# Sliding-window attention with a leaky-ReLU feed-forward: the probability adds go to the front of each step, the key placements behind

## The chip, the core and the metric

The kernel runs on one core of one Trainium2 chip. The core has five engines with a queue each: TensorE (PE, whose weight loads have a row of their own, PEld), VectorE (DVE), ScalarE (ACT), GpSimd (POOL) and SyncE (SP), which here only issues loads. An engine works through its queue in the order in which the program was written, and waits on semaphores for the others. The metric is the device time of one execution in microseconds (us). A profiled execution gives a span, from its first to its last instruction, and a device time that is a little longer.

## What is computed

Eight batches of eight heads attend over 576 tokens, each token to those at most 32 positions away. The heads are laid side by side into 4608 rows of 512, and these go through two matrix products with a leaky ReLU between.

```python
def _attn_ref(q, k, v):                       # 8, 8, 576, 64
    scores = np.matmul(q, k.transpose(0, 1, 3, 2)) / np.sqrt(D)
    mask = np.abs(pos[:, None] - pos[None, :]) <= 32
    scores = np.where(mask, scores, -1000000000.0)
    attn = np.exp(scores - np.max(scores, axis=-1, keepdims=True))
    attn = attn / (np.sum(attn, axis=-1, keepdims=True) + 1e-09)
    return np.matmul(attn, v)

def _moe_ref(x, w_in, w_out):                 # 4608x512, 512x2048, 2048x512
    h = x @ w_in
    return np.maximum(0.01 * h, h) @ w_out
```

## The kernel before, in words

Two heads make a pair, so a batch has four pairs (p = 0 to 3). The work on attention is cut into 64 units, numbered i: batch b = i // 8, half of the tokens hf = (i // 4) % 2, pair p = i % 4. For every unit there are three stages.

- `score(i)`: five matmuls of PE into the one PSUM tile `ps`, with the pair's keys as weights (`kbd`) and its queries `qT` streaming; then ACT takes the exponential into `e`, and POOL multiplies by the band mask into `pr`.
- `join(i)`: two instructions of DVE that add the two parts of `pr` into `both` (L239 and L241). Units below 12 have no join; their sums take two matmuls instead of one.
- `weighted(i)`: PE sums the probabilities into `s` (from `both`, L250) and forms the weighted values `x` (from `pr` and the block-diagonal values `vbd`, L262). Then DVE takes the reciprocal of `s` (L268, `r`) and multiplies it into `x` (L270), which gives a piece of `xT`. `s` and `x` have one PSUM buffer each.

A batch reaches that form in steps that belong to the batch before it. q and k are loaded by SP, cast to bf16 (`cast_qk`, into `qb` and `kb`), transposed by six small matmuls of PE into `tp` (L185), and copied out by ACT to `qT` (L193) and `kT` (L199). Two copies of DVE, one for each head of the pair, then place `kT` into the block-diagonal `kbd` (L202). `kbd` and `vbd` have two buffers, for even and odd batches; `kT` has two. `transposes(b)` is a generator of eight pieces (q0, k0, q1, k1, ...), and a piece of k ends with its placement.

The feed-forward is two kinds of tile: `h_tile(g, f)`, four matmuls (L281) and a leaky ReLU by ACT, over 288 tokens; and `o_tile(j)`, sixteen matmuls of 512 columns (L298) for 128 tokens, copied out by ACT and stored. Both take their PSUM tiles from a ring of four, which `tp` shares.

Nothing but the written order sets what stands behind what. `step()` writes one unit: a piece of the next batch's transposes, `score(i + 2)`, `weighted(i)`, `join(i + 1)`, another piece of the transposes, and then casts and loads for later batches. Which pieces, casts and loads belong to which unit of a batch is in the table `PLAN`. For batches from 2 on the last piece, k3, is transposed in the first unit of the batch itself, ahead of `score` and `weighted`; in batch 1 most of the pieces fall into its last units. A plan of due times puts the steps between the h and o tiles. Two stretches are written out by hand: the first batch, and the second one's preparation, which runs beside `h_tile(0, f)` and `h_tile(1, f)`. There the four query casts of batch 1 stand on DVE one after another, the key casts on POOL, and after every fourth `h_tile(1, f)` a pair's two pieces are transposed; `score(8)` and `score(9)` follow when all is done, and then the first o tile.

Of the kernel before, what the change touches and what calls it, by code (L numbers as in the profile page):

```python
# [10 lines left out]
BF16 = mybir.dt.bfloat16  # L11
# [5 lines left out]
def kernel(  # L17
# [12 lines left out]
    nc = tc.nc  # L30

    B, H, S, D = q.shape
# [5 lines left out]
    NPAIR = H // 2  # L38
# [9 lines left out]
    fload = ctx.enter_context(tc.tile_pool(name="fload", bufs=1))  # L48
    cast = ctx.enter_context(tc.tile_pool(name="cast", bufs=1))
    attn = ctx.enter_context(tc.tile_pool(name="attn", bufs=2))  # L50
    prob = ctx.enter_context(tc.tile_pool(name="prob", bufs=4))
    outp = ctx.enter_context(tc.tile_pool(name="outp", bufs=4))
    PS = bass.MemoryType.PSUM
# [8 lines left out]
    def load_qk(b, p, behind=None):  # L62


        for into, src, name in ((qf, q, "qf"), (kf, k, "kf")):
            t = fload.tile([96, 2, RUN * D], FP32, name=f"{name}{p}")
            if behind is not None:
                nc.sync.dma_start(out=t[0:1, 0, 0:1], in_=behind.bitcast(FP32))
                behind = None
            nc.sync.dma_start(  # L70
                out=t, in_=src[b, p:H:NPAIR].rearrange("a (p c) d -> p a (c d)", c=RUN),
            )
            into[b, p] = t
# [37 lines left out]
    kbd = [const.tile([128, NPAIR, NB, 128], BF16, name=f"kbd{i}") for i in range(2)]  # L111
    vbd = [const.tile([128, NPAIR, NB, 128], BF16, name=f"vbd{i}") for i in range(2)]
# [23 lines left out]
    for lo in (0, 64):  # L136
        w = win[lo:lo + 64]
        nc.gpsimd.affine_select(
            out=w, in_=w, compare_op=ALU.is_ge, fill=0.0,
# [3 lines left out]
            out=w, in_=w, compare_op=ALU.is_ge, fill=0.0,  # L143
# [20 lines left out]
    def cast_qk(b, p, q_eng=None):  # L164
        for eng, src, dst in ((q_eng or nc.gpsimd, qf, qb), (nc.gpsimd, kf, kb)):
            eng.tensor_copy(  # L166
                out=dst[:, p], in_=src[b, p].rearrange("p a (c d) -> p c a d", d=D),
            )

    def cast_v(b, p, on_act=False):  # L170
        for a in range(2):
            r = slice(64 * a, 64 * a + 64)
            if on_act:
                nc.scalar.activation(out=vbd[b % 2][r, p, :, r], in_=vf[b, p][r], func=AF.Copy)
            else:
                nc.gpsimd.tensor_copy(out=vbd[b % 2][r, p, :, r], in_=vf[b, p][r])  # L176

    def transposes(b):

        qT[b] = attn.tile([128, NPAIR, S], BF16, name="qT")  # L180
        for p in range(NPAIR):
            for which, src in (("q", qb), ("k", kb)):
                tp = mmps.tile([128, RUN, 96], BF16, name="tp", tag="mm")
                for c in range(RUN):
                    nc.tensor.transpose(  # L185
                        tp[:, c],
                        src[:, p, c].rearrange("p a d -> p (a d)"),
                        ident[0:96, 0:96],
                    )

                tok = tp.rearrange("p c i -> p i c")
                if which == "q":
                    nc.scalar.activation(  # L193
                        out=qT[b][:, p].rearrange("p (i c) -> p i c", c=RUN), in_=tok, func=AF.Copy,
                    )
                else:
                    kT = attn.tile([128, S], BF16, name="kT")
                    kT_v = kT.rearrange("p (i c) -> p i c", c=RUN)
                    nc.scalar.activation(out=kT_v, in_=tok, func=AF.Copy)  # L199
                    for a in range(2):  # L200
                        r = slice(64 * a, 64 * a + 64)
                        nc.vector.tensor_copy(  # L202
                            out=kbd[b % 2][r, p, :, r],
                            in_=kT[r].rearrange("p (n j) -> p n j", j=64),
                        )
                yield

    probs = {}

    def where(i):  # L210
        return i // 8, (i // 4) % 2, i % 4

    def score(i):
        b, hf, p = where(i)
        ps = scps.tile([128, 1024], FP32, name="ps")
        c0 = 512 - HALF
        for blk, q0, n in WIN[hf]:
            nc.tensor.matmul(  # L218
                ps[:, c0:c0 + n], kbd[b % 2][:, p, blk],
                qT[b][:, p, q0:q0 + n], start=True, stop=True,  # L220
            )
            c0 += n
        e = attn.tile([128, NCOL], BF16, name="e")
        nc.scalar.activation(  # L224
            out=e, in_=ps[:, 512 - HALF:512 - HALF + NCOL], func=AF.Exp, scale=scale,
        )
        pr = prob.tile([128, NCOL], BF16, name="pr")
        nc.gpsimd.tensor_mul(pr, e, mask[hf])  # L228
        probs[i] = pr, None

    def join(i):


        hf = where(i)[1]
        pr = probs[i][0]
        both = prob.tile([128, HALF], BF16, name="both")
        o0 = ODD[hf]
        o1 = o0 + NCOL - HALF
        nc.vector.tensor_add(both[:, o0:o1], pr[:, o0:o1], pr[:, HALF:NCOL])  # L239
        rest = slice(0, o0) if o0 else slice(o1, HALF)  # L240
        nc.vector.tensor_copy(out=both[:, rest], in_=pr[:, rest])  # L241
        probs[i] = pr, both

    def weighted(i):
        b, hf, p = where(i)
        pr, both = probs.pop(i)
        x = xps.tile([128, HALF], FP32, name="x")
        s = xps.tile([128, HALF], FP32, name="s")
        if both is not None:
            nc.tensor.matmul(s, ones_bd, both, start=True, stop=True)  # L250
        else:
            nc.tensor.matmul(
                s, ones_bd, pr[:, 0:HALF], start=True, stop=False, skip_group_check=True,
            )
            nc.tensor.matmul(
                s[:, ODD[hf]:ODD[hf] + NCOL - HALF], ones_bd, pr[:, HALF:NCOL],
                start=False, stop=True, skip_group_check=True,
            )
        c0 = 0
        for n_, (blk, q0, n) in enumerate(WIN[hf]):  # L260
            a = q0 - HALF * hf
            nc.tensor.matmul(  # L262
                x[:, a:a + n], vbd[b % 2][:, p, blk, :], pr[:, c0:c0 + n],
                start=(n_ == 0), stop=(n_ == len(WIN[hf]) - 1), skip_group_check=True,
            )
            c0 += n
        r = attn.tile([128, HALF], FP32, name="r")
        nc.vector.reciprocal(r, s)  # L268
        t0 = (b * S + hf * HALF) % RING
        nc.vector.tensor_mul(xT[:, p, t0:t0 + HALF], x, r)  # L270
# [43 lines left out]
    NC = 2 * NPAIR * B  # L314
    JOINED = 12
# [13 lines left out]
    def step_transposes(upto):  # L329
        while state["tp"] < min(upto, 8 * B):  # L330
            b = state["tp"] // 8
            if b not in t_parts:
                t_parts[b] = transposes(b)
            next(t_parts[b])
            state["tp"] += 1

    def step():


        i = state["done"]  # L340
        b, r = i // 8, i % 8
        if b > 0:
            upto = 8 * (b + 1) + PLAN[b > 1][0][r]
            step_transposes(max(upto - 1, 8 * (b + 1)))
        if i < 7:
            score(i + 1)
        elif 8 <= i < NC - 2:
            score(i + 2)
        weighted(i)
        if JOINED - 1 <= i < NC - 1:  # L350
            join(i + 1)
        if b > 0:
            step_transposes(upto)
        if 0 < b < B - 1:
            for p in PLAN[b > 1][1][r]:
                cast_qk(b + 1, p)
                if b + 2 < B:
                    load_qk(b + 2, p)
            for p in PLAN[b > 1][2][r]:
                cast_v(b + 1, p)  # L360
                if b + 2 < B:
                    load_v(b + 2, p)
        state["done"] += 1
# [11 lines left out]
    def load_w_out(i):  # L375
        c = slice(4 * i, 4 * i + 4)
        nc.gpsimd.dma_start(out=w_out_bf[:, c, :], in_=w_out_r[:, c, :])

    first = transposes(0)

    def first_pair():
        next(first)
        next(first)

    cast_qk(0, 0, nc.vector)
    make_masks()
# [35 lines left out]
    for f in range(FFC):  # L422
# [2 lines left out]
            step()  # L425
        if f % 4 == 3:
            nc.gpsimd.memset(kbd[1][:, f // 4], 0.0)
    for p in range(NPAIR):
        cast_qk(1, p, nc.vector)
    for p in range(NPAIR):  # L430
        load_v(1, p, w_out_bf[0:1, 4, 0:2] if p == 0 else None)
    second = transposes(1)
    for f in range(FFC):
        h_tile(1, f)
        if f % 4 == 3:
            next(second)
            next(second)
            nc.gpsimd.memset(vbd[1][:, f // 4], 0.0)
    state["tp"] = 16
    score(8)  # L440
    score(9)
    for p in range(NPAIR):
        load_qk(2, p)
# [71 lines left out]
```

## Time and profile before

| | |
|---|---|
| device time, three runs | 346.3, 348.11, 348.61 us; median 348.11 |
| the profiled execution | 348.38 us, its span 346.7 us |
| busy in that span | PE 319.2, DVE 228.2, ACT 200.2, POOL 180.5 us |
| costliest groups | `h_tile` matmuls 135.7 us, `o_tile` matmuls 130.3 us, reciprocals on DVE 125.3 us |

Times in rows of a trace are counted from the span's start. A row of the timeline has the start, the time from there to the end of the last of its instructions, the engine, line, operation and names, the count, and in brackets how long the engine had stood idle before it and what released it. A row of waits has who waited for whom, the total in us, how often, and the longest.

### The profile page before, as it was taken

The numbers are of one execution on the slowest core, as the hardware profiler recorded it, in microseconds if no ns is written. First come the engines' busy times: TensorE is split into PE (matmuls) and PEld (weight loads), VectorE is DVE, ScalarE is ACT, GpSimd is POOL, SyncE is SP. The second block draws the span as 40 slices with busy tenths as digits, with TensorE's granted clock in tenths as the row PEclk, the third lists the DMA queues.
The fourth block names the chain that finished last, engine by engine and source line by source line (L and its number), as shares of the span: only waits on it lengthen the run. The fifth ranks groups of instructions, "written<-read, shape, count | busy, mean of one in ns | idle before, by whom it ended". The sixth has DMA issues, their size and how long they took to land.

```text
span 346.7 us, 6990 instructions
## 1 busy us (share of the span) xinstructions
PE 319.2 (92%) x2703; PEld 217.0 (63%) x2725; DVE 228.2 (66%) x310; ACT 200.2 (58%) x432; POOL 180.5 (52%) x213
## 2 busy tenths in 40 slices
PE   2578969999999997999999997999999998899996
PEld 1346754576765856667675765767675765667663
DVE  5489541888767787587577877787586877766200
ACT  6765772375763936557474755658484656446441
POOL 7698557757845556355364637555463644221000
PEclk9999998999999999899999999999999999999999
DMA  8999989967774435263345433463211001010102
GB/s 184 206 199 225 268 182 232 248 164 203 175 165 135 133 96 138 69 188 74 112 126 161 134 82 106 115 183 84 80 51 61 32 2 61 2 61 3 61 2 91
DMA packets 60853, 42.40 MB, mean 122 GB/s; under 512 B 39700, under 2 KB 56340, under 8 KB 60820
## 3 DMA queue, kind: packets, MB, share of 16 engines
q1 hardware_dynamic: 51204, 28.32, 35.0%
q10 hardware_dynamic: 5328, 9.44, 7.6%
q0 software_dynamic: 4288, 4.20, 7.5%
q8 instruction: 21, 0.34, 0.4%
q14 instruction: 12, 0.10, 0.1%
HBM read 36.70 MB, written 9.44 MB: 133 GB/s over the span
## 4 chain that ended last, share of the span: by engine, by line
PE 78%; DVE 8%; DMA 7%; SPq 2%; ACT 2%; issue 1%; ACTq 0%; POOL 0%; DVEq 0%
PE mm L298 35%; PE mm L281 30%; DVE r L268 4%; DMA qf<-in_q_dram 4%; PE tp L185 4%; PE x L262 4%; PE ps L218 4%; DMA kf<-in_k_dram 2%; PE s L250 2%; SPq L70 1%; SPq L81 1%; DVE xT L270 1%; DVE kbd L202 1%; DVE both L241 1%; ACT kT L199 1%
## 5 line engine op out<-in xcount | busy, mean ns | idle before, releaser
L268 DVE RECIPROCAL r<-s 128x288 f32<-128x288 f32 x64 | 125.3, 1958 | 57.1 <-PE s L250 47.4
L228 POOL TENSOR_TENSOR pr<-e,mask 128x544 bf16<-128x544 bf16 x64 | 77.6, 1213 | 119.8 <-ACT e L224 73.4
L281 PE MATMUL mm<-xT,w_in_bf 128*128 128x288 bf16 x1024 | 135.7, 288 | 1.2 <-ACT kT L199 1.2
L298 PE MATMUL mm<-w_out_bf,gT 128*128 128x512 bf16 (+2 forms) x571 | 130.3, 376 | 1.3 <-issue 0.2
L281 PEld LDWEIGHTS <-w_in_bf 128*128 128x128 bf16 x1024 | 98.7, 99 | 27.0 <-issue 2.3
L285 ACT ACTIVATE gT<-mm 128x288 bf16<-128x288 f32 x256 | 99.6, 417 | 20.9 <-PE mm L281 9.8
L298 PEld LDWEIGHTS <-gT 128*128 128x128 bf16 x592 | 56.8, 99 | 61.0 <-issue 2.1
L303 ACT ACTIVATE o_sb<-mm 128x512 f32<-128x512 f32 (+2 forms) x37 | 21.7, 586 | 85.0 <-PE mm L298 85.0
L224 ACT ACTIVATE e<-ps 128x544 bf16<-128x544 f32 x64 | 39.9, 623 | 24.2 <-PE ps L218 12.3
L202 DVE COPY kbd<-kT 64x576 bf16<-64x576 bf16 x64 | 28.4, 444 | 22.0 <-ACT kT L199 21.5
L176 POOL CAST vbd<-vf 64x576 bf16<-64x576 f32 x58 | 39.2, 675 | 2.4 <-DMA vf<-in_v_dram 0.5
L270 DVE TENSOR_TENSOR xT<-x,r 128x288 bf16<-128x288 f32 x64 | 29.3, 458 | 6.7
L166 POOL CAST kb<-kf 96x768 bf16<-96x768 f32 x32 | 27.0, 844 | 11.4 <-DMA kf<-in_k_dram 11.4
L241 DVE COPY both<-pr 128x32 bf16<-128x32 bf16 x52 | 31.6, 608 | 0.0
L218 PE MATMUL ps<-qT,kbd 128*128 128x128 bf16 (+2 forms) x320 | 26.8, 217 | 1.4 <-ACT e L224 1.4
L262 PEld LDWEIGHTS <-vbd 128*128 128x128 bf16 x320 | 21.1, 99 | 10.7 <-issue 8.6
L262 PE MATMUL x<-pr,vbd 128*128 128x128 bf16 (+2 forms) x320 | 26.2, 214 | 0.9 <-DVE xT L270 0.8
L218 PEld LDWEIGHTS <-kbd 128*128 128x128 bf16 x320 | 20.6, 101 | 8.8 <-issue 1.5
L193 ACT ACTIVATE qT<-tp 128x576 bf16<-128x576 bf16 x32 | 20.8, 650 | 7.9 <-PE tp L185 7.4
L199 ACT ACTIVATE kT<-tp 128x576 bf16<-128x576 bf16 x32 | 20.9, 654 | 4.7 <-PE tp L185 1.7
L185 PE MATMUL tp<-ident,qb 96*128 96x96 bf16 x192 | 14.5, 215 | 8.6 <-DVE qb L166 8.6
L250 PE MATMUL s<-both,ones_bd 128*128 128x288 bf16 x52 | 14.9, 286 | 6.3 <-DVE both L241 6.3
(37 smaller groups left out, 131.5 us busy)
## 6 DMA issues: line engine op xcount, KB each, us to landing
qf<-in_q_dram SPq DMA_DIRECT2D x32, 288.0 KB, 3.4
kf<-in_k_dram SPq DMA_DIRECT2D x32, 288.0 KB, 4.2
vf<-in_v_dram SPq DMA_DIRECT2D x64, 144.0 KB, 3.6
out_dram<-o_sb ACTq DMA_DIRECT2D x35, 256.0 KB, 2.5
w_in_bf<-in_moe_w_in_dram POOLq DMA_DIRECT2D x8, 256.0 KB, 6.7
w_out_bf<-in_moe_w_out_dram POOLq DMA_DIRECT2D x4, 512.0 KB, 12.8
out_dram<-o_sb ACTq DMA_DIRECT2D x1, 192.0 KB, 1.9
out_dram<-o_sb ACTq DMA_DIRECT2D x1, 64.0 KB, 1.6
```

The lines of the kernel that those rows point to most:

```text
L176: nc.gpsimd.tensor_copy(out=vbd[b % 2][r, p, :, r], in_=vf[b, p][r])
L202: nc.vector.tensor_copy(out=kbd[b % 2][r, p, :, r], in_=kT[r].rearrange("p (n j) -> p n j", j=64),)
L218: nc.tensor.matmul(ps[:, c0:c0 + n], kbd[b % 2][:, p, blk], qT[b][:, p, q0:q0 + n], start=True, stop=True,)
L224: nc.scalar.activation(out=e, in_=ps[:, 512 - HALF:512 - HALF + NCOL], func=AF.Exp, scale=scale,)
L228: nc.gpsimd.tensor_mul(pr, e, mask[hf])
L241: nc.vector.tensor_copy(out=both[:, rest], in_=pr[:, rest])
L262: nc.tensor.matmul(x[:, a:a + n], vbd[b % 2][:, p, blk, :], pr[:, c0:c0 + n], start=(n_ == 0), stop=(n_ == len(WIN[hf]) - 1), skip_group_c ...
L268: nc.vector.reciprocal(r, s)
L270: nc.vector.tensor_mul(xT[:, p, t0:t0 + HALF], x, r)
L281: nc.tensor.matmul(h[:, 0:HALF], w_in_bf[:, c, ts(f, 128)], xT[:, c, ds(t0, HALF)], start=(c == 0), stop=(c == DMC - 1),)
L285: nc.scalar.activation(out=gT[:, f, ds(t0, HALF)], in_=h[:, 0:HALF], func=AF.Prelu, alpha=0.01,)
L298: nc.tensor.matmul(o[:, lo:hi], gT[:, f, ds(128 * j % RING, 128)], w_out_bf[:, f, lo:hi], start=(f == 0), stop=(f == FFC - 1),)
```

## The change

`place_keys()` is new: a piece of k no longer ends with the two copies into `kbd` but puts its `kT` on a list, and `place_keys` writes the copies of all that is on the list. `kT` gets four buffers. In `step()` the order becomes: `join(i + 1)`, `place_keys()`, a piece of transposes, `score(i + 2)`, `weighted(i)`, `place_keys()`, the other piece.

In the second batch's preparation the casts of pairs 0 and 1 stay ahead of `h_tile(1, 0)`; those of pairs 2 and 3 move behind the placements of pairs 0 and 1. Since `cast_qk` casts q on DVE and k on POOL, a `memset` of `vbd[1]` on POOL now stands ahead of the last key cast. `score(8)` moves from the end to behind `h_tile(1, 11)`.

```diff
+    kt = ctx.enter_context(tc.tile_pool(name="kt", bufs=4))
...
-                    kT = attn.tile([128, S], BF16, name="kT")
+                    kT = kt.tile([128, S], BF16, name="kT")
...
-                    for a in range(2):
-                        r = slice(64 * a, 64 * a + 64)
-                        nc.vector.tensor_copy(
-                            out=kbd[b % 2][r, p, :, r],
-                            in_=kT[r].rearrange("p (n j) -> p n j", j=64),
-                        )
+                    unplaced.append((b, p, kT))
                 yield
+
+    unplaced = []
+
+    def place_keys():
+
+        while unplaced:
+            b, p, kT = unplaced.pop(0)
+            for a in range(2):
+                r = slice(64 * a, 64 * a + 64)
+                nc.vector.tensor_copy(
+                    out=kbd[b % 2][r, p, :, r],
+                    in_=kT[r].rearrange("p (n j) -> p n j", j=64),
+                )
...
         b, r = i // 8, i % 8
+        if JOINED - 1 <= i < NC - 1:
+            join(i + 1)
+        place_keys()
         if b > 0:
...
         weighted(i)
-        if JOINED - 1 <= i < NC - 1:
-            join(i + 1)
+        place_keys()
         if b > 0:
             step_transposes(upto)
...
     def first_pair():
         next(first)
         next(first)
+        place_keys()
...
-    for p in range(NPAIR):
-        cast_qk(1, p, nc.vector)
+    cast_qk(1, 0, nc.vector)
+    cast_qk(1, 1, nc.vector)
...
         h_tile(1, f)
         if f % 4 == 3:
+            p = f // 4
             next(second)
             next(second)
-            nc.gpsimd.memset(vbd[1][:, f // 4], 0.0)
+            place_keys()
+            if p + 2 < NPAIR:
+                cast_qk(1, p + 2, nc.vector)
+            nc.gpsimd.memset(vbd[1][:, p], 0.0)
+        if f == 11:
+            score(8)
     state["tp"] = 16
-    score(8)
     score(9)
```

The first place is DVE's queue around unit 24, the first of batch 3. The rows below are of the kernel before: the end of `weighted(23)`, `join(24)`, the placement of k3 into `kbd1`, `weighted(24)`, `join(25)`, and the reciprocal of unit 25. The numbers behind names only tell tiles apart.

```order
L270 TENSOR_TENSOR xT_142<-x_1889,r_1897 128x288
L239 TENSOR_TENSOR both_1900<-pr_1820 128x256
L241 COPY both_1900<-pr_1820 128x32
L202 COPY kbd1_126<-kT_1942 64x9x64 x2
L268 RECIPROCAL r_1964<-s_1957 128x288
L270 TENSOR_TENSOR xT_142<-x_1956,r_1964 128x288
L239 TENSOR_TENSOR both_1967<-pr_1887 128x256
L241 COPY both_1967<-pr_1887 128x32
L268 RECIPROCAL r_2036<-s_2029 128x288
```

The same place in the changed kernel, where line numbers are 9 or 10 higher and tiles have other numbers: the end of `weighted(23)`, `join(25)`, `weighted(24)`, the placement, `join(26)`, the reciprocal of unit 25.

```order
L279 TENSOR_TENSOR xT_145<-x_1895,r_1903 128x288
L248 TENSOR_TENSOR both_1938<-pr_1893 128x256
L250 COPY both_1938<-pr_1893 128x32
L277 RECIPROCAL r_1968<-s_1961 128x288
L279 TENSOR_TENSOR xT_145<-x_1960,r_1968 128x288
L212 COPY kbd1_129<-kT_1948 64x9x64 x2
L248 TENSOR_TENSOR both_2021<-pr_1958 128x256
L250 COPY both_2021<-pr_1958 128x32
L277 RECIPROCAL r_2042<-s_2035 128x288
```

What moved: the placement went from ahead of the reciprocal of unit 24 to behind its product, and the join there is that of the unit after next.

The second place is the second batch's preparation, on DVE, before: the last product of batch 0, four query casts, and the placements of the four pairs.

```order
L270 TENSOR_TENSOR xT_142<-x_519,r_528 128x288
L166 CAST qb_123<-qf0_363 96x768
L166 CAST qb_123<-qf1_368 96x768
L166 CAST qb_123<-qf2_372 96x768
L166 CAST qb_123<-qf3_376 96x768
L202 COPY kbd1_126<-kT_624 64x9x64 x2
L202 COPY kbd1_126<-kT_668 64x9x64 x2
L202 COPY kbd1_126<-kT_712 64x9x64 x2
L202 COPY kbd1_126<-kT_756 64x9x64 x2
```

And DVE at that place now.

```order
L279 TENSOR_TENSOR xT_145<-x_522,r_531 128x288
L167 CAST qb_126<-qf0_366 96x768
L167 CAST qb_126<-qf1_371 96x768
L212 COPY kbd1_129<-kT_623 64x9x64 x2
L167 CAST qb_126<-qf2_375 96x768
L212 COPY kbd1_129<-kT_669 64x9x64 x2
L167 CAST qb_126<-qf3_379 96x768
L212 COPY kbd1_129<-kT_715 64x9x64 x2
L212 COPY kbd1_129<-kT_769 64x9x64 x2
```

The placements of pairs 0 and 1 no longer stand behind the casts of pairs 2 and 3.

At the same place on POOL, before: key casts, the clearing of `vbd1`, the masks of units 8 and 9, and the first two pairs' value casts.

```order
L166 CAST kb<-kf_374 96x768
L166 CAST kb<-kf_378 96x768
L438 MEMSET vbd_128 128x1152 x4
L228 TENSOR_TENSOR pr<-e,mask_140 128x544 x2
L176 CAST vbd_128<-vf_571 64x9x64 x2
L176 CAST vbd_128<-vf_575 64x9x64 x2
```

And POOL there now.

```order
L167 CAST kb<-kf_377 96x768
L454 MEMSET vbd_131 128x1152
L167 CAST kb<-kf_381 96x768
L454 MEMSET vbd_131 128x1152 x2
L237 TENSOR_TENSOR pr<-e,mask_143 128x544
L454 MEMSET vbd_131 128x1152
L237 TENSOR_TENSOR pr<-e,mask_143 128x544
L177 CAST vbd_131<-vf_570 64x9x64 x2
L177 CAST vbd_131<-vf_574 64x9x64 x2
```

One clearing stands between the last two key casts, and the mask of unit 8 ahead of the last clearing.

## The prediction

> **What bounds the kernel now.** I read the page first: the span, the busy times, the granted clock in 40 slices, and the chain of waits by engine.
>
> ```profile
> span 346.7 us, 6990 instructions
> PE 319.2 (92%) x2703; PEld 217.0 (63%) x2725; DVE 228.2 (66%) x310; ACT 200.2 (58%) x432; POOL 180.5 (52%) x213
> ...
> PEclk9999998999999999899999999999999999999999
> ...
> PE 78%; DVE 8%; DMA 7%; SPq 2%; ACT 2%; issue 1%; ACTq 0%; POOL 0%; DVEq 0%
> ```
>
> PE carries 78% of the chain, so time can come only from PE's idle 27.5 us (346.7 - 319.2) or from stretches where its clock is low: the two slices with an 8 (slices of 8.67 us, so from 52 and from 139 us). Next the waits between 92 and 326 us, where the kernel is in its steady run; of PE's only one is long.
>
> ```profile
> PE s L250 <- DVE both L241: 6.3, 3, 2.1
> ```
>
> Three times PE waits 2.1 us for a join. DVE is busy for only 66% of the span, so it has time enough; three times the wrong thing stands first in its queue. The other idle time that the change can touch lies around the second batch (part 3).
>
> **Part 1: the join and the placement in a step.** The timeline around the first of the three, units 24 and 25:
>
> ```profile
> 130.06 0.40 PE L218 MATMUL ps<-qT,kbd 128*128 128x96 bf16 x5
> 130.30 0.29 PE L250 MATMUL s<-both,ones_bd 128*128 128x288 bf16 x1
> 134.09 0.40 PE L218 MATMUL ps<-qT,kbd 128*128 128x96 bf16 x5
> 136.59 0.28 PE L250 MATMUL s<-both,ones_bd 128*128 128x288 bf16 x1 [2.09 <-DVE both L241]
> ...
> 131.07 0.65 ACT L199 ACTIVATE kT<-tp 128x576 bf16<-128x576 bf16 x1 [0.47 <-PE x L262]
> ...
> 127.51 1.21 POOL L228 TENSOR_TENSOR pr<-e,mask 128x544 bf16<-128x544 bf16 x1 [3.02 <-issue]
> ...
> 131.75 0.91 DVE L202 COPY kbd<-kT 64x576 bf16<-64x576 bf16 x2 [2.32 <-ACT kT L199]
> 132.69 1.96 DVE L268 RECIPROCAL r<-s 128x288 f32<-128x288 f32 x1
> ...
> 135.13 0.28 DVE L239 TENSOR_TENSOR both<-pr 128x256 bf16<-128x256 bf16 x1
> 135.33 1.21 DVE L241 COPY both<-pr 128x32 bf16<-128x32 bf16 x1
> 136.91 1.96 DVE L268 RECIPROCAL r<-s 128x288 f32<-128x288 f32 x1 [0.37 <-PE s L250]
> ```
>
> The sum of unit 24 was there from 130.30, but DVE's queue held the placement, which waited for ACT's `kT` until 131.72. So the reciprocal began at 132.69, the join of unit 25 ended at 136.54, and PE stood.
>
> Now with the new order. The mask product for unit 25 ends at 127.51 + 1.21 = 128.72. Its join, which now stands in front, takes 0.20 to the start of its second instruction and 1.21 for that, at the longest seen here, so it is done by 130.2. The reciprocal follows the sum by 0.32 (136.59 to 136.91): 130.62. From a reciprocal's start to the next thing after the product are 2.44 (132.69 to 135.13): the two placements run from 133.06 to 133.97. `score(27)`, which needs them, came at 134.09, 0.12 later. So the cover of the late placement is thin, and I cost it at nothing with a bound of 0.5 us each (an instruction of DVE more ahead of it). The join of unit 25 is then long done, and PE's wait is gone. `join(26)` ends by 135.4 (133.97 + 0.20 + 1.21), up to 0.7 after the reciprocal of unit 25 could begin; PE next asks for that product in unit 26, a step later, so this lies beside PE's tiles. Gain: 3 x 2.09 = **6.3 us**.
>
> Does the join in front cost anything elsewhere? Only where a mask product comes later than the sum of the unit before. The tightest of units 12 to 62, by going through them all, is at the end:
>
> ```profile
> 310.61 1.21 POOL L228 TENSOR_TENSOR pr<-e,mask 128x544 bf16<-128x544 bf16 x1 [2.84 <-ACT e L224]
> ...
> 312.91 0.29 PE L250 MATMUL s<-both,ones_bd 128*128 128x288 bf16 x1
> ```
>
> It ends at 311.82, 1.09 ahead of the sum. So the joins stay hidden by PE's own work. DVE's order is otherwise as it was: reciprocal, product, join.
>
> **Part 2: the clock after a stall.** The table by stretches, 2 us each, in the two low slices of the clock. Its columns are the length, the busy time and count of PE, PEld, DVE, ACT and POOL, then the granted clock, the DMA share and GB/s:
>
> ```profile
> 52.00:54.00 2.00, 1.78 (x6) 0.71 (x5) 0.08 (x1) 0.62 (x1) 2.00 (x3) 0.50 1.36 193
> 54.00:56.00 2.00, 2.00 (x8) 0.81 (x7) 0.00 (x0) 0.00 (x0) 1.94 (x4) 0.70 1.06 239
> 136.00:138.00 2.00, 1.41 (x16) 1.12 (x16) 1.63 (x2) 0.49 (x1) 2.00 (x3) 0.78 0.77 243
> 138.00:140.00 2.00, 2.00 (x10) 1.30 (x9) 1.61 (x4) 0.98 (x3) 0.04 (x1) 0.50 0.83 216
> 140.00:142.00 2.00, 2.00 (x16) 1.50 (x15) 0.00 (x0) 1.23 (x3) 0.00 (x0) 0.87 0.31 79
> ```
>
> The lost clock is 1.41 x 0.22 + 2 x 0.50 + 2 x 0.13 = **1.6 us** here and 1.78 x 0.50 + 2 x 0.30 = **1.5 us** at 52 to 56, which part 3 includes. Both follow an idle PE, and there is no third after 22 us, though the other two stalls of 2.1 us drew none. Without the idle time I take both back; the other end is nothing.
>
> The Trainium skill ("TensorE: Matmul & The Clock Gate", Part 1) says that the clock halves after an idle window of some 3.4 us and that the window runs freely. The 0.50 agrees; the stall of 2.09 us is shorter than that window, and the trace lowers the clock all the same, once in three.
>
> **Part 3: the second batch.** The timeline from 45.98 to 59.21, engine by engine, and at the end four rows of the chain of waits in order of time (start, time, what):
>
> ```profile
> 45.98 1.64 PE L281 MATMUL mm<-xT,w_in_bf 128*128 128x288 bf16 x12
> 48.83 0.65 PE L281 MATMUL mm<-xT,w_in_bf 128*128 128x288 bf16 x4 [1.22 <-ACT kT L199]
> 51.64 0.51 PE L218 MATMUL ps<-qT,kbd 128*128 128x96 bf16 x5 [1.41 <-ACT e L224]
> 51.95 0.63 PE L298 MATMUL mm<-w_out_bf,gT 128*128 128x512 bf16 x1
> ...
> 59.21 0.40 PE L262 MATMUL x<-pr,vbd 128*128 128x96 bf16 x5
> ...
> 48.12 0.65 ACT L199 ACTIVATE kT<-tp 128x576 bf16<-128x576 bf16 x1 [1.54 <-DVE kbd L202]
> ...
> 46.63 0.56 DVE L166 CAST qb<-qf 96x768 bf16<-96x768 f32 x1 [2.95 <-DMA qf<-in_q_dram]
> 47.11 2.78 DVE L202 COPY kbd<-kT 64x576 bf16<-64x576 bf16 x6
> ...
> 48.02 0.82 POOL L166 CAST kb<-kf 96x768 bf16<-96x768 f32 x1 [2.37 <-DMA kf<-in_k_dram]
> 48.79 4.05 POOL L438 MEMSET vbd<- 128x1152 bf16 x4
> 52.81 2.38 POOL L228 TENSOR_TENSOR pr<-e,mask 128x544 bf16<-128x544 bf16 x2
> 55.13 2.83 POOL L176 CAST vbd<-vf 64x576 bf16<-64x576 f32 x4
> ...
> 46.38 5.50 SPq L81 DMA_DIRECT2D vf<-in_v_dram  x8
> ...
> 52.80 6.10 PE mm L298 x22
> 59.61 2.59 PE mm L298 x12
> 121.45 0.26 PE tp L185 x6
> 121.71 0.49 PE mm L281 x4
> ```
>
> DVE's fourth cast waits for its load until 46.63, with all placements behind it; so ACT has no free `kT` until 48.02, and PE's last h tile waits 1.22. Then `score(9)` waits 1.41 for the exponential of `score(8)`, since there is one `ps`.
>
> Now, piece by piece on PE from 45.98 on: `score(8)` 0.24 (130.06 to 130.30), four h tiles of 0.49, 1.96, so 48.18; q3's transposes 0.26, 48.44. Those of k3 need POOL's last key cast, which waits for its load as before: 48.02 + 0.82 = 48.84, a wait of 0.4 that stays. Then 0.26 and `score(9)` 0.24: the first o tile begins at 49.35 instead of 51.95, 2.6 earlier. The clearing of 1.01 us (4.05 / 4), newly ahead of that key cast, lies in POOL's wait of 2.37, and no load moves in SP's queue.
>
> Up to unit 8 PE has 1 and 22 recorded matmuls of 512 columns, 24 in groups of four. At full clock one takes 2.59 / 12 = 0.216 (here 6.10 / 22 = 0.277), so 5.2 us: 54.55. Unit 8's score (0.24) and two sums stand ahead of its `x`, 0.5 as an estimate from that: 55.0 against 59.21. But POOL is late next: 48.84, two clearings to 50.87, the mask of unit 8 to 52.06, a clearing to 53.07, the mask of unit 9 to 54.26, and a pair's two value casts (2.83 / 2) to 55.7. Their loads, issued from 46.38 on, are not late: the casts show no wait for them. `x` waits for them, 0.7. It stands at 55.7, so of 4.2 us there remain 59.21 - 55.7 = **3.5 us**.
>
> **The sum.** 6.3 + 1.6 + 3.5 = 11.4 us. From the profiled execution's 348.38 us (span 346.7 and 1.7 around it) that gives **337.0 us**, a span of 335.3. That execution lies 0.3 above the median of 348.11.
>
> **The rivals.** *The clock does not come back.* If the two dips belong to the place and not to the idle time, 1.6 and 1.5 stay: 340.1 us. For it: two stalls just as long drew no dip. Against it: both dips begin right behind a stall, and none lies elsewhere. Chance 0.10. The Trainium skill's rule of a whole idle window (the page above) speaks for it at 136 us.
>
> *The late placement becomes the wait.* With only 0.12 us to spare, `score` would wait three times for up to 0.5: 338.5 us. For it: nothing else covers the placement. Chance 0.12.
>
> *The second batch gains nothing*, since the loads of q3 and k3 end it anyway: 340.5 us. For it: POOL's 48.02. Against: 1.41 of the wait comes from `ps`, after the loads. Chance 0.06.
>
> *Slower: the join blocks the reciprocal.* DVE would stand at the join for POOL while a sum lies ready, at every one of the 52 joins. To undo the gain it must cost over 11.4 / 52 = 0.22 us a step; at 0.29, 15 us in all, the time is 352 us. Even the tightest mask product would have to end 1.09 + 0.22 later than now. Chance 0.03. The Trainium skill (the same page, on the array's architecture) says that DVE's queue is strictly first in, first out; the placement that held up a ready sum until 131.75 agrees.
>
> **How the numbers follow.** The rest, 0.69, is for the sum. Its own bounds: with the waits for k3 (0.4) and `vbd` (0.7) gone as well, 335.9, and runs before lay 1.8 below the median at least once. The range is 335.3 to 340.2, which leaves out the third rival, the slower one and a little on both sides. A difference under 1%, 3.5 us, is about what a measurement cannot tell from none. All cases but the slower one lie at 340.5 or below, 2.2% faster: faster 0.94, same 0.03, slower 0.03.
>
> **What would show it.** In the changed profile: no wait of a sum for `both`; no 8 in the clock's row; the first o matmul near 49.4 us; a wait of `x` for `vbd` near 55 us; the reciprocal of unit 24 about 0.3 behind its sum, with the placement after the product. I am wrong if `score` waits for `kbd` after each odd batch's first unit, or if DVE stands idle ahead of joins with sums lying ready.

## The result, and the profile after

The changed kernel takes 338.93 us (median of 4 runs, 338.24 to 339.75), the kernel before 347.94 us on the same chip (4 runs, 346.3 to 348.61). The ratio is 0.9749, its 95% interval 0.9705 to 0.9792. The forecast was 337.0 us in a range of 335.3 to 340.2: the direction and the range held, and 1.9 us of the gain did not come. The profiled execution took 338.24 us, against 348.38 before. Of all runs told of below one, of 349.23 us, was in a slower state of the chip, and its ratio leaves it out.

From the page of the changed kernel: the span, the busy times, the granted clock in 40 slices and the chain of waits by engine.

```profile
span 336.5 us, 7011 instructions
...
PE 317.7 (94%) x2725; PEld 215.6 (64%) x2725; DVE 232.6 (69%) x310; ACT 199.9 (59%) x432; POOL 180.3 (54%) x213
...
PEclk9999999999999999999999999999999999999999
...
PE 83%; DMA 6%; DVE 5%; SPq 2%; ACT 2%; POOL 1%; issue 1%; ACTq 0%; DVEq 0%
```

No slice has an 8 any more, and PE's idle time fell from 27.5 to 18.8 us. PE's share of the chain rose from 78% to 83%. Between 90 and 318 us the list of waits has no row for PE at all; for DVE it has these two (who waited for whom, total, times, longest):

```profile
DVE r L277 <- PE s L259: 44.7, 41, 2.4
DVE both L248 <- POOL pr L237: 0.9, 5, 0.2
```

DVE now waits for sums, and almost never at a join. The timeline around units 24 and 25, PE first and then DVE:

```profile
128.34 0.41 PE L227 MATMUL ps<-qT,kbd 128*128 128x96 bf16 x5
128.58 0.29 PE L259 MATMUL s<-both,ones_bd 128*128 128x288 bf16 x1
...
132.37 0.40 PE L227 MATMUL ps<-qT,kbd 128*128 128x96 bf16 x5
132.61 0.29 PE L259 MATMUL s<-both,ones_bd 128*128 128x288 bf16 x1
...
137.75 0.42 PE L186 MATMUL tp<-ident,kb 96*128 96x96 bf16 x6
...
127.03 0.71 DVE L248 TENSOR_TENSOR both<-pr 128x256 bf16<-128x256 bf16 x1 [0.19 <-POOL pr L237]
128.90 1.96 DVE L277 RECIPROCAL r<-s 128x288 f32<-128x288 f32 x1 [1.07 <-PE s L259]
131.34 0.90 DVE L212 COPY kbd<-kT 64x576 bf16<-64x576 bf16 x2
```

The reciprocal of unit 24 starts 0.32 behind its sum, at 128.90. The placement ends at 132.24, and `score(27)`, which needs it, starts at 132.37: 0.13 us to spare. The sum of unit 25 follows its score without a gap.

To see where the 10.2 us of span came from, the same places are set beside each other. From the kernel before, PE's rows that the prediction did not show:

```profile
71.17 3.59 PE L281 MATMUL mm<-xT,w_in_bf 128*128 128x288 bf16 x28
...
143.39 0.42 PE L185 MATMUL tp<-ident,kb 96*128 96x96 bf16 x6
```

From the changed one, the second batch on PE:

```profile
48.73 5.34 PE L307 MATMUL mm<-w_out_bf,gT 128*128 128x512 bf16 x24
...
54.84 0.41 PE L271 MATMUL x<-pr,vbd 128*128 128x96 bf16 x5 [0.29 <-POOL vbd L177]
...
61.52 0.40 PE L227 MATMUL ps<-qT,kbd 128*128 128x64 bf16 x5 [1.25 <-ACT e L233]
...
68.76 0.28 PE L259 MATMUL s<-both,ones_bd 128*128 128x288 bf16 x1 [0.77 <-DVE r L277]
69.33 0.41 PE L271 MATMUL x<-pr,vbd 128*128 128x64 bf16 x5 [0.28 <-DVE xT L279]
69.58 2.61 PE L290 MATMUL mm<-xT,w_in_bf 128*128 128x288 bf16 x20
```

| place on PE | before | after | earlier by |
|---|---|---|---|
| `x` of unit 8 | 59.21 | 54.84 | 4.37 |
| h tiles behind unit 12 | 71.17 | 69.58 | 1.59 |
| `score(26)` | 130.06 | 128.34 | 1.72 |
| sum of unit 25 | 136.59 | 132.61 | 3.98 |
| transposes of k in the next unit | 143.39 | 137.75 | 5.64 |
| end of the span | 346.7 | 336.5 | 10.2 |

Read downwards: the second batch brings 4.4 us and gives 2.8 back by the h tiles behind unit 12; the first of the three stalls brings 3.98 - 1.72 = 2.26, its low clock 5.64 - 3.98 = 1.66, and the other two stalls 10.2 - 5.64 = 4.56. So Parts 1 and 2 came, and most of Part 3 was lost between unit 8 and unit 12.

The 4.4 us are the gain over this one execution of the kernel before, with its low clock at 52 us. Two more traces below have the old second batch (the kernel before with its stores on SP, and with longer stalls). Both have a full clock there, and `x` of unit 8 at 56.99 and 56.84; against these the 54.84 is only 2.2 and 2.0 us earlier.

ACT's rows between unit 8 and unit 12 (ACTq is the issue of a DMA from ACT's queue), and one row of the chain of waits (start, time, what):

```profile
52.39 0.60 ACT L312 ACTIVATE o_sb<-mm 128x512 f32<-128x512 f32 x1 [2.09 <-PE mm L307]
55.81 0.37 ACTq L313 DMA_DIRECT2D out_dram<-o_sb  x1
56.28 0.62 ACT L233 ACTIVATE e<-ps 128x544 bf16<-128x544 f32 x1 [3.30 <-POOL vbd L177]
57.01 0.60 ACT L312 ACTIVATE o_sb<-mm 128x512 f32<-128x512 f32 x1
60.41 0.34 ACTq L313 DMA_DIRECT2D out_dram<-o_sb  x1
60.85 0.62 ACT L233 ACTIVATE e<-ps 128x544 bf16<-128x544 f32 x1 [3.24 <-DMA kf<-in_k_dram]
...
50.34 5.40 DMA vf<-in_v_dram
```

The first o tile was copied out by 52.99, but its store went out only at 55.81, and the next exponential stood behind it on ACT. The second store waited from 57.61 to 60.41. In the chain a load of v that lands at 55.74 releases the first store; for the second the bracket behind it names a load of k. A store has no use for either: it reads `o_sb`. The order of ACT's queue, with the semaphores that its rows wait for, tells why:

```order
L312 ACTIVATE o_sb<-mm 128x512 [waits PE_49]
L313 DMA out_dram<-o_sb 128x512 [waits DMAHW1_49,Activation_49]
L233 ACTIVATE e<-ps 128x544 [waits PE_49,Pool_49]
L312 ACTIVATE o_sb<-mm 128x512 [waits PE_49]
L313 DMA out_dram<-o_sb 128x512 [waits DMAHW5_49,Activation_49]
```

And from SP's queue the load of k that has the second one's semaphore:

```order
L71 DMA kf_790<-in_k_dram 96x2x384 [waits DMAHW5_49,Pool_49]
```

The loads of SP and the stores of ACT take the same eight DMA semaphores (DMAHW0 to 7) in turn, and a transfer is issued only when the one that had its semaphore before has landed. Store 0 has DMAHW1 after the last value load of batch 1, store 1 has DMAHW5 after a key load of batch 2. In the kernel before, the tiles came 4.8 and 4.4 us later, and the loads had all but landed:

```profile
57.21 0.60 ACT L303 ACTIVATE o_sb<-mm 128x512 f32<-128x512 f32 x1 [4.34 <-PE mm L298]
57.92 0.38 ACTq L304 DMA_DIRECT2D out_dram<-o_sb  x1
...
61.38 0.60 ACT L303 ACTIVATE o_sb<-mm 128x512 f32<-128x512 f32 x1 [1.51 <-PE mm L298]
62.75 0.34 ACTq L304 DMA_DIRECT2D out_dram<-o_sb  x1
```

There the stores stood 0.1 and 0.8 us behind their tiles. The semaphores fell otherwise there: by the trace the first store was issued behind the first query load of batch 2, which landed at 57.84, and the second behind the third, which landed at 62.67. The loads moved forward too, but less than the tiles: the key load that the second store now waits for landed at 61.46 before and lands at 60.33 now. The late exponential also reaches unit 12. POOL and DVE of the changed kernel, and the last sum on PE ahead:

```profile
64.21 0.30 PE L261 MATMUL s<-pr,ones_bd 128*128 128x288 bf16 x1
...
64.23 2.38 POOL L237 TENSOR_TENSOR pr<-e,mask 128x544 bf16<-128x544 bf16 x2
...
65.48 1.29 DVE L248 TENSOR_TENSOR both<-pr 128x256 bf16<-128x256 bf16 x1 [0.77 <-POOL pr L237]
66.77 1.94 DVE L277 RECIPROCAL r<-s 128x288 f32<-128x288 f32 x1
```

`join(12)`, the first join, stands ahead of the reciprocal of unit 11. POOL was late with its probabilities, so a sum whose matmuls began at 64.21 got its reciprocal only at 66.77, and PE waited 0.77 and 0.28 us at unit 12.

### The profile page after: what moved, and what is told of

Same layout as the page of the kernel before. It is cut to its first block, busy times and chain, and to the rows that moved or that the text cites. A ratio compares the mean times of both kernels' runs of the same rounds, so it can differ in the third digit from the quotient of the medians.

```text
span 336.5 us, 7011 instructions
## 1 busy us (share of the span) xinstructions
PE 317.7 (94%) x2725; PEld 215.6 (64%) x2725; DVE 232.6 (69%) x310; ACT 199.9 (59%) x432; POOL 180.3 (54%) x213
## 4 chain that ended last, share of the span: by engine, by line
PE 83%; DMA 6%; DVE 5%; SPq 2%; ACT 2%; POOL 1%; issue 1%; ACTq 0%; DVEq 0%
PE mm L290 36%; PE mm L307 33%; PE tp L186 4%; PE x L271 4%; PE ps L227 4%; DVE r L277 3%; DMA kf<-in_k_dram 2%; DMA out_dram<-o_sb 2%; PE s L259 2%; DMA vf<-in_v_dram 2%; SPq L82 1%; SPq L71 1%; DVE xT L279 1%; ACT kT L200 0%; POOL vbd L177 0%
## 5 line engine op out<-in xcount | busy, mean ns | idle before, releaser
L290 PE MATMUL mm<-xT,w_in_bf 128*128 128x288 bf16 x1024 | 133.9, 286 | 0.0
L167 POOL CAST kb<-kf 96x768 bf16<-96x768 f32 x32 | 27.5, 860 | 9.3 <-DMA kf<-in_k_dram 9.3
L248 DVE TENSOR_TENSOR both<-pr 128x256 bf16<-128x256 bf16 x52 | 27.0, 519 | 3.9 <-POOL pr L237 2.1
L250 DVE COPY both<-pr 128x32 bf16<-128x32 bf16 x52 | 24.6, 473 | 0.0
```

Of the source, the lines that this page charges most:

```text
L290: nc.tensor.matmul(h[:, 0:HALF], w_in_bf[:, c, ts(f, 128)], xT[:, c, ds(t0, HALF)], start=(c == 0), stop=(c == DMC - 1),)
```

## The experiments

The theory after the result: the written order of the steps gives the three stalls and the clock (some 8.5 us); the second batch gives 4.4, of which ACT's stores and `join(12)` take 2.8 back. Rivals: the steps' order alone made it all; the low clock belongs to the place, not to the stall; the stores only show a wait that something else causes. Each time is set against the kernel before on the same chip. That took 346.39 us (17 runs) for the steps alone, the second batch alone, the stores held back and `join(12)` behind its unit; 347.24 (11 runs) for the stores on SP with and without `join(12)`, the changed kernel again and the joins in front; 346.72 (17 runs) for the kernel before with its stores on SP, the late placements and the longer stalls.

**The steps alone.** The second batch is written as before; the new order in the steps and the four `kT` buffers stay.

```diff
-    cast_qk(1, 0, nc.vector)
-    cast_qk(1, 1, nc.vector)
+    for p in range(NPAIR):
+        cast_qk(1, p, nc.vector)
...
-            if p + 2 < NPAIR:
-                cast_qk(1, p + 2, nc.vector)
-            nc.gpsimd.memset(vbd[1][:, p], 0.0)
-        if f == 11:
-            score(8)
+            nc.gpsimd.memset(vbd[1][:, f // 4], 0.0)
     state["tp"] = 16
+    score(8)
```

> The new order in the steps alone (and four buffers for the transposed keys); the second batch's casts, clearing and score(8) stand as before. Theory: the parts add up. The three waits of a sum for its join are gone (6.3 us, as they measured 2.25 each between the two traces 6.8), and with them the low clock behind the first (1.6); the low clock behind the second batch's idle time stays. So about 8 us less than before, near 340.0 us. Rival: the changed kernel's gain hangs on the second batch coming earlier; then this one gains clearly less, 343 or more.

Measured 340.11 us (339.61 to 340.94), 0.9819 [0.9779, 0.9858] of before, no wait of PE between 90 and 318 us, and the clock's row all 9. Most of the gain is the steps', 6.3 us by the medians. What was not looked for: the first o matmul stood at 49.83 here, 2.1 earlier than in the profile before, though the casts were where they had been. With four `kT` buffers the wait of 1.22 for a free one is gone. The h tiles behind unit 12 came at 71.21 all the same, and this is where it went:

```profile
63.15 0.40 PE L227 MATMUL ps<-qT,kbd 128*128 128x64 bf16 x5 [1.99 <-ACT e L233]
```

**The second batch alone.** Steps as before: the placement right after each piece, the join behind the product.

```diff
             next(t_parts[b])
+            place_keys()
             state["tp"] += 1
...
-        if JOINED - 1 <= i < NC - 1:
-            join(i + 1)
-        place_keys()
...
         weighted(i)
-        place_keys()
+        if JOINED - 1 <= i < NC - 1:
+            join(i + 1)
```

> The second batch's new order alone; in the steps the keys are placed right after their transposes and the join stands behind the product, as before. Theory: 1.6 us less than before at the first h tile of the third half (71.2 us before), so 346.5 us, with three waits of a sum for its join of 2.1 us left, and a low clock behind some of them. Rival, as forecast: 3.5 us less, 344.5 us.

Measured 346.25 us (343.81 to 348.07, 10 runs), 0.999 [0.9957, 1.0023]: no gain that can be told. In the trace the h tiles behind unit 12 come at 69.22, 1.95 earlier than before, and the span is 2.0 shorter, but runs with stalls differ among themselves by 4 us, so the comparison neither shows nor excludes it. The list of waits and the stretch behind the first stall (length, busy time and count of PE, PEld, DVE, ACT, POOL, clock, DMA, GB/s):

```profile
PE s L259 <- DVE both L250: 6.3, 3, 2.1
...
136.00:138.00 2.00, 2.00 (x10) 1.30 (x9) 1.66 (x4) 0.96 (x4) 0.09 (x1) 0.50 0.76 212
```

The three stalls are back, and with the first the low clock. There is no dip at 52 us, but that alone shows no cause: the trace of the longer stalls has the old second batch, PE waits there of 0.81 and 1.41 us, and no dip either.

**The stores held back.** The stores of o tiles 0 to 2 are issued behind that of tile 3, still from ACT.

```diff
-            nc.scalar.dma_start(out=out[ts(j, 128), lo:hi], in_=o_sb[:, lo:hi])
+            held.append((j, lo, hi, o_sb))
+            while j >= 3 and held:
+                j_, lo_, hi_, t_ = held.pop(0)
+                nc.scalar.dma_start(out=out[ts(j_, 128), lo_:hi_], in_=t_[:, lo_:hi_])
```

> The changed kernel with the stores of the first three o tiles put behind the fourth's on ACT's queue. Theory: ACT stood behind these stores from 53.0 to 55.8 and from 57.6 to 60.4 us, since each waits until an earlier load on its DMA semaphore has landed, and the exponentials of units 10 and 11 stood behind them; without that PE loses the waits of 1.25 us (score for e) and most of 1.05 (sum and x of unit 12): the h tiles start near 67.6 instead of 69.6, and the time falls by about 2 us to 336.3. Rival: DVE's reciprocals and POOL's masks set this stretch, and the time stays within 0.5 us of 338.2.

Measured 338.05 us (336.9 to 339.83), 0.9761 [0.9723, 0.9798]: hardly less than the changed kernel. ACT, then PE:

```profile
65.70 3.49 ACTq L318 DMA_DIRECT2D out_dram<-o_sb  x4
69.30 0.62 ACT L233 ACTIVATE e<-ps 128x544 bf16<-128x544 f32 x1 [3.00 <-DMA vf<-in_v_dram]
...
66.10 2.12 PE L290 MATMUL mm<-xT,w_in_bf 128*128 128x288 bf16 x16
70.28 1.63 PE L290 MATMUL mm<-xT,w_in_bf 128*128 128x288 bf16 x12 [2.05 <-ACT gT L294]
```

The h tiles start at 66.10, 3.5 earlier than in the changed kernel, so the gain is there up to this place. But held stores take later semaphores, and wait for later loads, of batch 2: the four of them hold ACT for 3.5 us, and PE waits 2.05 for `gT`. The wait was moved, not removed.

**`join(12)` behind its unit.** Only the first join goes back behind the product.

```diff
-        if JOINED - 1 <= i < NC - 1:
+        if JOINED <= i < NC - 1:
             join(i + 1)
...
         weighted(i)
+        if i == JOINED - 1:
+            join(i + 1)
```

> The changed kernel with join(12), the first, behind weighted(11) as it was before; all other joins in front. Theory: at this one place the join in front holds up a ready sum (the reciprocal of unit 11 began 2.1 us after it could), and PE's waits of 0.77 and 0.28 us at unit 12 come from that: they go, 1.0 us less, 337.2. Rival: the join then ends as late, since its mask product is late, and the sum of unit 12 waits for it instead: within 0.5 us of 338.2.

Measured 337.07 us (336.8 to 339.0), 0.974 [0.9702, 0.9777]. The waits of 0.77 and 0.28 at unit 12 are gone, the one for `e` (1.55 here) stays. By the trace it is worth the 1 us; the runs alone could not tell that.

**The stores of the first four tiles from SP.** One line of the changed kernel, then the same with the edit above, and the changed kernel itself on this chip.

```diff
-            nc.scalar.dma_start(out=out[ts(j, 128), lo:hi], in_=o_sb[:, lo:hi])
+            store = nc.sync if j < 4 else nc.scalar
+            store.dma_start(out=out[ts(j, 128), lo:hi], in_=o_sb[:, lo:hi])
```

> The changed kernel with the stores of the first four o tiles issued from SP's queue, which holds nothing that PE soon needs, instead of ACT's. Theory: no exponential stands behind a store any more; the wait of score for e (1.25 us) and those of unit 12 (0.77 and 0.28) go, and none comes at the h tiles, as it did where the four stores went in one block behind the fourth tile: the h tiles start near 66.6 us, 3 us earlier than in the changed kernel, and the time is 335.5. Rival: stores that run beside the loads slow these down and POOL's value casts with them: within 1 us of the changed kernel.

> The same with join(12) behind weighted(11) as well. Theory: where the stores no longer hold up the exponentials, the mask product of unit 12 is early and the join in front costs nothing, so this equals the kernel with the stores on SP's queue alone within 0.5 us. Rival: the two add up, another 1 us less.

> The changed kernel once more, on the same chip as the others of this group, for comparison: 338 us.

| | us | ratio to before | first o matmul to the h tiles behind unit 12 |
|---|---|---|---|
| changed kernel again | 339.2 (338.67 to 339.74) | 0.9778 [0.9740, 0.9815] | 49.22 to 70.65 |
| stores on SP | 335.61 (334.99 to 336.09) | 0.9674 [0.964, 0.9708] | 49.83 to 67.44 |
| the same, `join(12)` behind | 335.0 (334.39 to 336.07) | 0.966 [0.9625, 0.9694] | 48.22 to 66.35 |

This settles it: 3.6 us come back with nothing changed but the queue that issues four stores, and the stretch shrinks from 21.4 to 17.6 us. With the stores on SP, ACT goes on right behind its copy and waits only for scores:

```profile
53.48 0.60 ACT L312 ACTIVATE o_sb<-mm 128x512 f32<-128x512 f32 x1 [2.09 <-PE mm L307]
55.51 0.62 ACT L233 ACTIVATE e<-ps 128x544 bf16<-128x544 f32 x1 [1.43 <-PE ps L227]
```

PE's waits of 1.25, 0.77 and 0.28 are all gone; so those at unit 12 came from the stores, and the edit of `join(12)` adds only 0.6 us, inside the spread. Either version beats both kernels.

**The stores from SP in the kernel before.** The same line there.

> The kernel before with the stores of the first four o tiles issued from SP's queue. Theory: before, the first store began 0.1 us after its tile was ready and the second 0.8, since the o tiles came 2.6 us later and the loads had landed by then: a gain of 0 to 0.8 us, the same within what can be measured. Rival: the stores on SP are a gain of their own: 3 us, as in the changed kernel.

Measured 345.93 us (343.58 to 349.23, 12 runs), 0.9968 [0.9935, 1.0001]: no difference to be told, though a gain of up to 0.65% is not excluded. In the profile before the stores hardly waited, but this does not make the wait the change's own. The kernel with longer stalls (below) is, up to unit 24 and but for one `memset`, the kernel before, and its trace shows the wait as well. The stretch behind 52 us with its clock, PE, then ACT:

```profile
52.00:54.00 2.00, 2.00 (x11) 0.89 (x10) 0.00 (x0) 0.07 (x1) 2.00 (x2) 1.00 1.40 190
...
56.84 0.40 PE L263 MATMUL x<-pr,vbd 128*128 128x96 bf16 x5
...
64.13 0.40 PE L219 MATMUL ps<-qT,kbd 128*128 128x64 bf16 x5 [1.86 <-ACT e L225]
...
54.84 0.60 ACT L307 ACTIVATE o_sb<-mm 128x512 f32<-128x512 f32 x1 [2.77 <-PE mm L302]
58.34 0.38 ACTq L308 DMA_DIRECT2D out_dram<-o_sb  x1
```

The clock is full at 52 us, so the first tile is copied out by 55.44, and its store stands there until 58.34; the second waits 3.1 us. From `x` of unit 8 to the h tiles behind unit 12 are 13.96 us here (56.84 to 70.80), and 11.96 with the stores on SP (56.99 to 68.95). So in this trace the stores cost the kernel before 2.0 us too. In the profile before its low clock had put off the tiles until the loads had landed. In the changed kernel the stretch is 14.74 us in its first trace and 15.78 in its second, with some 1.05 us of waits at unit 12, behind `join(12)`, in both.

**Half of the new order.** First only the joins in front, the placement right after each piece; then only the placement late, the join behind the product.

```diff
             next(t_parts[b])
+            place_keys()
             state["tp"] += 1
```

> The changed kernel with the joins in front, but every placement right behind its transposes, so k3's stands ahead of the reciprocal of a batch's first unit as before. Theory: the join is early, but the reciprocal is still late (132.69 in the trace before), and the next unit's sum and product need its PSUM tiles back: some 0.8 us of the 2.1 us wait remain at units 25, 41 and 57, as a wait for the reciprocal or the product: 2.4 us above the changed kernel. Rival: the join in front was all that counted: equal to it within 0.5 us.

```diff
-        if JOINED - 1 <= i < NC - 1:
-            join(i + 1)
         place_keys()
...
         weighted(i)
+        if JOINED - 1 <= i < NC - 1:
+            join(i + 1)
         place_keys()
```

> The changed kernel with each join behind the product as before, and only the placements moved. Theory: at unit 24 the reciprocal is early, but the placement now stands behind join(25), which ends 0.5 to 1.5 us after the product; score(27), due 0.12 us after the placement would end, and the sum of unit 25 wait for 0.3 to 1.3 us at each of the three places: 1 to 4 us above the changed kernel's 339.2. Rival: the late placement was all that counted: equal to it within 0.5 us.

Measured 341.58 us (340.67 to 342.43), 0.9847 [0.9804, 0.9891], for the joins, and 341.39 (340.42 to 342.42), 0.986 [0.9822, 0.9897], for the placements: 2.4 and 2.2 us above the changed kernel's 339.2, which for the second was measured on another chip. PE's waits in the steady run, of the first and then of the second:

```profile
PE x L271 <- DVE xT L279: 0.9, 3, 0.3
PE s L259 <- DVE r L277: 0.6, 3, 0.2
```

```profile
PE ps L227 <- DVE kbd L212: 2.6, 3, 1.1
```

Either half takes the stall of 2.1 away and leaves a smaller one: with the placement ahead of the reciprocal, PE waits 0.2 and 0.3 us in the next unit; with the join behind the product and so ahead of the placement, the placement comes up to 1.06 us too late for `score`. Only together do they leave PE no wait.

**Longer stalls.** The kernel before, with one more reciprocal of 288 columns on DVE, into a scratch tile, ahead of that of units 24, 40 and 56.

```diff
+        if i in (24, 40, 56):
+            idle = const.tile([128, HALF], FP32, name=f"idle{i}")
+            nc.vector.reciprocal(idle, ones_f)
         r = attn.tile([128, HALF], FP32, name="r")
```

> The kernel before with one more reciprocal of 288 columns on DVE, into a scratch tile, ahead of that of units 24, 40 and 56, so that PE's three waits of 2.1 us become 4.0. Theory: the low clock comes from the idle time, and more surely the longer it is: two or three of the three stalls draw it, each some 1.6 us; the time is 3 x 1.96 = 5.9 us plus 1.6 to 3.2 more above before: 355 us. Rival: the dip belongs to the place at unit 25 and not to idle time: one dip as before, 353 us.

Measured 353.98 us (352.96 to 354.68), 1.0221 [1.0183, 1.0258]. That time lies between what the two theories give, so the trace has to tell: the list of waits, and the stretches behind the three stalls.

```profile
PE s L251 <- DVE both L242: 10.2, 3, 3.7
...
138.00:140.00 2.00, 2.00 (x20) 1.46 (x19) 1.86 (x1) 1.06 (x2) 0.00 (x0) 0.66 0.88 263
140.00:142.00 2.00, 2.00 (x10) 1.30 (x9) 0.84 (x4) 0.82 (x2) 0.00 (x0) 0.50 0.07 24
220.00:222.00 2.00, 2.00 (x19) 1.47 (x18) 1.83 (x1) 1.06 (x2) 0.00 (x0) 0.64 0.90 251
222.00:224.00 2.00, 2.00 (x11) 1.24 (x9) 0.86 (x4) 0.82 (x2) 0.00 (x0) 0.51 0.14 37
...
302.00:304.00 2.00, 2.00 (x19) 1.60 (x17) 1.90 (x4) 1.64 (x4) 0.00 (x0) 1.00 0.03 8
```

The stalls are 3.69, 3.69 and 2.86 us long. The place at 220 us, which had no low clock in any trace with a stall of 2.1, has one behind 3.69, and it costs as much as the first: 2 x 0.36 + 2 x 0.49 = 1.7 us. All four runs have a mean granted clock of 0.985 to 0.990, where the 17 runs of the kernel before on that chip go from 0.989 to 1.000. So the low clock comes from the idle time; the place alone does not make it.

## Why the prediction was right, and where it was off

**Part 1 was right.** No wait of a sum is left. The 6.3 us became 6.8: the brackets of 2.09 count from a modelled end of the last matmul, and the next one would have started before that end. From the start of `score(27)` to that of the sum are 2.50 us before and 0.24 now, 2.26 each.

**The cover of the late placement held**, though as thin as forecast: 0.13 us to spare against 0.12. The bound of 0.5 us for the case that it fails was not put to the test; with a whole join ahead of the placement, as in the kernel with late placements alone, `score` waited up to 1.06.

**Part 2 was right for the execution that it was read from**: 1.66 us against 1.6 behind the first stall, and no dip at 52 us. The rival that the clock stays low is refuted at the first stall by the changed trace and by the longer stalls. The dip at 52 us proves less, since two traces with the old second batch have none. The Trainium skill ("TensorE: Matmul & The Clock Gate", Part 1) has the clock fall after one idle window of some 3.4 us. Two of the three longer stalls exceed that and drew the dip, the third, 2.86, did not, as the rule has it; but the stall of 2.09 at 136 us drew it too, and there the measurement decides.

**That the number came so close is in part luck.** The forecast takes 3.1 us for two stretches of low clock from one execution, and not every execution has them. The mean granted clock tells: 0.990 in that execution with two dips, 0.994 in the two other traces with one, 0.999 and more without. Of the 45 runs of the kernel before on the three chips, 19 have 0.999 or more. On the first chip these are ten of 17, and they take 344.63 to 346.46 us, the other seven 346.8 to 348.39. Of the ten runs of the changed kernel three have 0.995, so it is not quite free of dips, though its two traces show none. So the size of the gain hangs on the runs that it is set against: 2.5% with four runs of the kernel before, 2.2% (0.9778) in the repetition with eleven.

**Part 3 failed in one step.** Against the profile before, the gain up to `x` of unit 8 was even larger than forecast, 4.37 for 3.5: the first o matmul at 48.73 instead of 49.4, and the wait for `vbd` 0.29 instead of 0.7. The step that failed is the next, "so of 4.2 us there remain 59.21 - 55.7 = **3.5 us**": it takes everything behind unit 8 to follow at the old distance, and says of the loads only that "no load moves in SP's queue". No load changed its place there, but ACT's stores moved against them: their tiles came 4.8 and 4.4 us earlier, the loads of batch 2 only 0.9 to 1.2, and so the stores had to wait, with the exponentials behind them. (Without the low clock at 52 us they wait in the old order too, as the trace of the longer stalls shows.) So 1.7 us stayed of 4.4, and the sum became 6.8 + 1.7 + 1.7 = 10.2 instead of 11.4. With the stores out of ACT's queue, the stretch from `x` of unit 8 to the h tiles takes what it took in the profile before, 11.96 us (55.48 to 67.44; 59.21 to 71.17), and those h tiles come 3.7 earlier than there. But not all of the 3.5 belongs to the new order: 1.5 of it was the low clock at 52 us. Where both kernels have their stores on SP and a full clock at that place, `x` of unit 8 stands at 56.99 and 55.48 and the h tiles at 68.95 and 67.44, so the order of the second batch is worth 1.5 us, by one trace each.

**The slower rival** did happen, once. At `join(12)` DVE stood at a join with a sum ready, and PE lost 1.05 us; the cause was the late exponential. The look through the joins had begun at unit 12, where the steady run begins, and the kernel's first join, written ahead of unit 11's reciprocal, was left out of it.

**What stays open:** why 2.1 us of idle PE lowers the clock at one place of a trace and not at the two others, and in some executions and not in others. The cost of the stores adds up: in the repeated run of the changed kernel the brackets of PE that are gone with the stores on SP were 0.28, 1.85, 0.78 and 0.28, in sum 3.2. If each counts some 0.16 too little, as in Part 1, that makes 3.8, which is by how much the stretch shrank (21.43 to 17.61).

## What to carry to other kernels

Where work is drawn forward, look at every queue that issues transfers, also one whose place in the order did not change: a store on a computing engine waits for a DMA semaphore that an earlier, unrelated load may hold, and everything behind it on that engine waits too. In a queue that works in order, what is ready early and needed late goes to the front, and what is needed last goes behind; here it took both halves, and each alone left a smaller wait. An idle PE can cost more than its idle time, so look at the clock's row behind each stall, and at the clock of several runs before a dip is counted as a gain.

## What the runs showed of the hardware

- A store issued from ACT stood 2.8 us for a load that SP had issued, twice (52.99 to 55.81, 57.61 to 60.41), since both take DMA semaphores from one set of eight. The kernel with longer stalls, where this place is as before the change, shows it too (2.9 and 3.1 us). Issued from SP, the four stores cost PE nothing that a row shows.
- The granted clock fell to 0.50 behind stalls of 3.69 us (both), behind that of 2.09 at 136 us, and not behind 2.86 us at 300 us; each fall cost 1.6 to 1.7 us. It does not come in every execution: 19 of 45 runs of the kernel before, whose trace shows three stalls of 2.1 us, have a mean granted clock of 0.999 or more.
